# Batches 1 to 7 in units of all tokens by half of the expert features, with fixed engine orders and small pieces of work in the gaps

## The chip, the core and the metric

The kernel runs on one core of one Trainium2 chip. The metric is the device time of one execution in microseconds (us), from the first to the last instruction; the median of the runs is given. TensorE (PE) multiplies matrices and writes to PSUM, VectorE (DVE) does elementwise arithmetic, ScalarE (ACT) does activation functions and copies, GpSimd (POOL) and SyncE (SP) are used here for issuing DMA transfers. Every engine has a queue of its own and works through it in order; engines wait for one another by semaphores.

## The reference

An attention block with 8 batches and 8 heads (512 tokens, 32 states, 64 features a head) makes 544 rows of 512 per batch; an expert block with 2048 features follows. All is float32 on the chip (the expert weights come as float64 and are converted there).

```python
scores = scale * np.matmul(x, state.transpose(0, 1, 3, 2))       # tokens read states
a = softmax(scores); xread = np.matmul(a, state)
scores2 = scale * np.matmul(state, x.transpose(0, 1, 3, 2))      # states read tokens
a2 = softmax(scores2); sread = np.matmul(a2, x)
attn = np.concatenate([xread, sread], axis=2)                     # (8, 8, 544, 64)
x = attn.transpose(0, 2, 1, 3).reshape(4352, 512)
h = x @ w_in                                                      # (4352, 2048)
sp = np.maximum(h, 0.0) + np.log1p(np.exp(-np.abs(h)))            # softplus
g = h * erf(sp)
return g @ w_out                                                  # (4352, 512)
```

## The kernel before

For tokens, h is computed as (a) times (state x w_in): the small product `m` = state x w_in ("mixing") is made per batch, so that the contraction has only 256 (8 heads x 32 states). Batch 0 is done with plain products while the weights arrive; batches 1 to 7 and the state rows (called batch 8 here) use the seven-product scheme of Strassen and Winograd, at both products. The core below is that of batches 1 to 7. A batch has four passes: two halves of the tokens (h) by two halves of the features (g). One pass of `hidden7` takes 256 of the 512 tokens as a 2x2 block scheme whose blocks have 128 tokens, so each of its matmuls has 128 columns:

```python
def hidden7(b, g, h, between, copy=nc.scalar.copy):
    hs = act.tile([P, 4, S], F32, name="hs")
    s = act.tile([P, 4, S], F32, name="s")
    c11, c12, c21, c22 = (hs[:, k] for k in range(4))
    m1, u2, u3 = s[:, 3], c12, c21
    def product(n, bank, first=True):
        x, y = X[b, g][n - 1], Ys[b][n - 1]
        for i in range(GF):                                   # GF = 4 blocks of 128 features
            q = slice(P * i, P * i + P)
            ...  # matmul(out=bank[:, q], lhsT=x[:, q], rhs=y[:, h])     128 x 128
    p, q = (ps_h.tile([P, S], F32, name="h") for _ in range(2))
    product(1, p);  copy(m1, p)
    product(6, q);  add(u2, m1, q)
    between()
    product(2, p, False);  copy(c11, p)
    product(7, q, False);  add(u3, m1, q);  softplus(0)
    between()
    p, q = (ps_h.tile([P, S], F32, name="h") for _ in range(2))
    product(5, p);  add(c22, u3, p)
    product(4, q);  add(c21, u3, q)
    between()
    marks[:] = product(3, p, False), add(c12, u2, p)
    for k in (3, 2, 1):
        softplus(k)
    return s, hs

def finish(s, hs, parts=(slice(0, GF),)):
    nc.scalar.activation(out=s, in_=s, func=ACTF.Erf)
    for k in parts:
        nc.vector.tensor_tensor(s[:, k], s[:, k], hs[:, k], op=ALU.mult)
```

`between()` puts a piece of the pass before, its second product, between the pieces of the first. That second product (`project7`, matmuls of 256 columns) adds the two feature halves up in PSUM, over two passes, and `store7` evicts after the second:

```python
def project7(gT, hs, g, first, last, acc, order=range(7)):
    ...  # four VectorE sums of 128x512, 7 products of 4 matmuls 128x256,
         # accumulated in acc[0..3] over the two passes (first, last)

def store7(acc, put):
    ...  # 1 ScalarE copy, 2 VectorE adds of 128x512 and 3 of 128x256, 3 transfers out
```

The attention of the next batch is a generator that is stepped at set places of the passes. Its transposed scores, its weights and a transposed copy of x (`xT`) have tiles of their own; `w_in` (all 8 pieces) stays on chip. The order on VectorE and ScalarE in batches 1 to 8 is chosen by the scheduler (batch 0 is fixed by `in_order`).

Of the kernel before, what the change touches and what calls it, by code (L numbers as in the profile page):

```python
# [16 lines left out]
def kernel(  # L17
# [17 lines left out]
    nc = tc.nc  # L35
# [29 lines left out]

    x_t = {}
# [11 lines left out]
    def in_order(begun):  # L78

        last = {}  # L80
        for i in nc.cur_bb.bb.instructions[begun:]:
            if i.engine in last:
                tc.add_manual_dep(i, last[i.engine].name, mybir.DependencyInfo(
                    mybir.DependencyClass.NoSync, mybir.DependencyReason.DATA), reason="in_order")
            if i.engine in (nc.tensor.engine, nc.vector.engine, nc.scalar.engine,
                            nc.sync.engine):
                last[i.engine] = i
# [34 lines left out]
    w_in = const.tile([P, NF // 2, NK, 2 * P], F32, name="w_in")  # L122
# [31 lines left out]
    def weights_in(j):  # L154
        return weight(w_in[:, j],
                      moe_w_in[:, 2 * P * j:2 * P * j + 2 * P].rearrange("(k p) f -> p k f", p=P),
                      (NK, 2 * P))
# [32 lines left out]
    def scored(b, xT):  # L190


        s2 = [ps_at.tile([P, S], F32, name="at") for _ in range(2)]
# [8 lines left out]
    def scores(b, xT):  # L202
        s2 = scored(b, xT)
        on_pe = marks.pop()
        sc = att.tile([P, 2, S], F32, name="sc")
        for e in range(2):
            last = nc.scalar.copy(sc[:, e], s2[e])
        marks[:] = last, on_pe
        return sc, last
# [127 lines left out]
    def turn_x(b):  # L337
        xT = att.tile([P, NI, S], F32, name="xT")
        last = nc.vector.transpose(out=xT.rearrange("p i t -> p (i t)"),
                                   in_=xq_t.pop(b).rearrange("p i m d -> p (i m d)"))  # L340
        if b + 1 < B:
            load_xq(b + 1)
        return xT, last

    def attention(b, xT=None):

        turned = []
        if xT is None:  # L350
            xT, *turned = turn_x(b)
        sc, _ = scores(b, xT)
        marks.extend(turned)
        yield
        both = att.tile([P, NI, S], F32, name="xT")
        a = states_weights(b, [sc[:, e] for e in range(2)], both)
        yield
        if b == 2:
            z1 = sums(a)
        else:  # L360
            m2 = largest(sc)
            yield
            z2 = weigh_tokens(sc, m2, both[:, 2:4])
            yield
            z1 = sums(a)
            inverse(z2)
            yield
        normalise(a, z1)
        for e in range(2):
            nc.vector.transpose(out=aT[b][:, e], in_=both[:, e])  # L370
        yield
        if b == 2:
            z2 = weigh_tokens(sc, largest(sc), both[:, 2:4])
            inverse(z2)

        nc.vector.transpose(out=both[:, 0:2], in_=both[:, 2:4])
        a2T = att.tile([P, 2, NC, P], F32, name="sc")
        blocks = both[:, 0:2].rearrange("p e (c m n) -> p m (e c) n", m=NI, n=Ns)
        rows = a2T.rearrange("p e c (i n) -> p i (e c) n", n=Ns)
        for m in range(NI):  # L380
            for i in range(NI):
                nc.sync.dma_start(out=rows[Ns * m:Ns * m + Ns, i],
                                  in_=blocks[Ns * i:Ns * i + Ns, m])
        yield
        read_tokens(b, a2T, z2, *((ps_h, "h") if 1 < b < B - 1 else ()))
        if b + 1 < B:
            load_x(b + 1)
        yield
# [8 lines left out]
    def mixed_pair(b, gs):  # L397

        for g in gs:
            m_t[b, g] = mix.tile([P, 2, gw], F32, name="m")  # L400
        ps = [[pool.tile([P, gw], F32, name=n) for _ in range(2)]
              for pool, n in ((ps_at, "at"), (ps_h, "h"))]
        for k, g in enumerate(gs):
            for i in range(NI):
                for e in range(2):
                    r, q = slice(D * e, D * e + D), slice(Ns * i, Ns * i + Ns)
                    nc.tensor.matmul(out=ps[k][e][q, :], lhsT=st[r, b, q],  # L407
                                     rhs=w_in[r, 2 * g:2 * g + 2, i, :], start=True, stop=True)
        for k in 0, 1:
            nc.scalar.copy(m_t[b, gs[k]][:, 0], ps[k][0])  # L410
            nc.vector.tensor_copy(m_t[b, gs[k]][:, 1], ps[k][1])

    def mixed_part(b, g, j, parts, copy0=nc.scalar.copy, copy1=nc.vector.tensor_copy):
        n = gw // parts
        mg = m_t[b, g][:, :, n * j:n * j + n]
        fs = slice(2 * g + j, 2 * g + j + 2 // parts)
        ps = [ps_at.tile([P, gw], F32, name="at")[:, 0:n] for _ in range(2)]
        for i in range(NI):
            for e in range(2):
                r, q = slice(D * e, D * e + D), slice(Ns * i, Ns * i + Ns)  # L420
                nc.tensor.matmul(out=ps[e][q, :], lhsT=st[r, b, q],  # L421
                                 rhs=w_in[r, fs, i, :], start=True, stop=True)
# [3 lines left out]
    def combine_m(b, g):  # L426
# [4 lines left out]
        S1, S2, S4 = (sx[:, k] for k in range(3))  # L431
        tt = nc.vector.tensor_tensor
        tt(S1, X21, X22, op=ALU.add)
        tt(S2, S1, X11, op=ALU.subtract)
        tt(X21, X11, X21, op=ALU.subtract)
        tt(S4, X12, S2, op=ALU.subtract)
        X[b, g] = X11, X12, S4, X22, S1, S2, X21

    def combine_s(g):


        (X11, X12), (X21, X22) = ([w_in[:, GF * g + 2 * j:GF * g + 2 * j + 2, 2 * k:2 * k + 2, :]
# [5 lines left out]
        tt(S1, X21, X22, op=ALU.add)  # L448
        tt(S2, S1, X11, op=ALU.subtract)
        tt(X21, X11, X21, op=ALU.subtract)  # L450
        tt(S4, X12, S2, op=ALU.subtract)
        X[B, g] = X11, X12, S4, X22, S1, S2, X21

    def combine_a(b):
# [9 lines left out]
        tt(T1, Y12, Y11, op=ALU.subtract)  # L464
        tt(T2, Y22, T1, op=ALU.subtract)
        tt(Y12, Y22, Y12, op=ALU.subtract)
        last = tt(T4, Y21, T2, op=ALU.subtract)
        Ys[b] = Y11, Y21, Y22, T4, T1, T2, Y12
        return last
# [3 lines left out]
    def hidden7(b, g, h, between, copy=nc.scalar.copy):  # L473
# [4 lines left out]
        hs = act.tile([P, 4, S], F32, name="hs")  # L478
        s = act.tile([P, 4, S], F32, name="s")
        c11, c12, c21, c22 = (hs[:, k] for k in range(4))  # L480
        m1, u2, u3 = s[:, 3], c12, c21

        def product(n, bank, first=True):
            x, y = X[b, g][n - 1], Ys[b][n - 1]
            for i in range(GF):
                q = slice(P * i, P * i + P)
                if b < B:
                    ops = [(x[:, q], y[:, h])]
                else:
                    ops = [(x[:, i // 2, k, P * (i % 2):P * (i % 2) + P], y[:, k])  # L490
                           for k in range(2)]
                for k, (lhsT, rhs) in enumerate(ops):
                    last = nc.tensor.matmul(out=bank[:, q], lhsT=lhsT, rhs=rhs,  # L493
                                            start=(first and i == 0 and k == 0),
                                            stop=(i == GF - 1 and k == len(ops) - 1),
                                            skip_group_check=not first)
            return last

        def softplus(k):
            nc.scalar.activation(out=s[:, k], in_=hs[:, k], func=ACTF.Softplus)  # L500
        add = lambda o, x, y: nc.vector.tensor_tensor(o, x, y, op=ALU.add)  # L501
        p, q = (ps_h.tile([P, S], F32, name="h") for _ in range(2))
        product(1, p)
        copy(m1, p)  # L504
        product(6, q)
        add(u2, m1, q)
        between()
        product(2, p, False)
        copy(c11, p)  # L509
        product(7, q, False)  # L510
        add(u3, m1, q)
        softplus(0)
        between()
        p, q = (ps_h.tile([P, S], F32, name="h") for _ in range(2))
        product(5, p)
        add(c22, u3, p)
        product(4, q)
        add(c21, u3, q)
        between()
        marks[:] = product(3, p, False), add(c12, u2, p)  # L520
        for k in (3, 2, 1):
            softplus(k)
        return s, hs

    def hidden(b, fts, copies=(nc.vector.tensor_copy,) * 4):

        hs = act.tile([P, 4, S], F32, name="hs")
        s = act.tile([P, 4, S], F32, name="s")  # L530
        banks = []
        for i, f in enumerate(fts):
            hp = ps_h.tile([P, S], F32, name="h")
            for e in range(2):
                on_pe = nc.tensor.matmul(
                    out=hp, lhsT=m_t[b, f // GF][:, e, P * (f % GF):P * (f % GF) + P],
                    rhs=aT[b][:, e], start=(e == 0), stop=(e == 1))
            banks.append((nc.scalar.activation(out=s[:, i], in_=hp, func=ACTF.Softplus),
                          copies[i](hs[:, i], hp), on_pe))
        return s, hs, banks  # L540

    def finish(s, hs, parts=(slice(0, GF),)):
        nc.scalar.activation(out=s, in_=s, func=ACTF.Erf)  # L543
# [59 lines left out]

    def store7(acc, put):
        twice = lambda t: t.unsqueeze(1).to_broadcast([P, 2, E2])
        two = lambda t: t.rearrange("p (c e) -> p c e", c=2)
        m1, u3 = (outs.tile([P, E2], F32, name=n) for n in ("m1", "u3"))
# [13 lines left out]
    def put_x(b, h):  # L621
        rows = out[TB * b:TB * b + S].rearrange("(c p) e -> c p e", p=P)

        def go(r, ot, c=slice(0, d_model)):
            nc.sync.dma_start(out=rows[2 * h + r][:, c], in_=ot[:, c])
# [16 lines left out]

    def fast(b, parts, put):
        for h in range(parts):
            box = []

            def project_(gT, k, g, h, box):
                if k == 0:
                    box.extend(tiles(4))
                yield from project7(*gT, g, k == 0, k == 1, box,  # L650
# [361 lines left out]
```

## Time and profile before

| | before |
|---|---|
| median of 3 runs | 732.25 us (732.15 to 732.46) |
| span of the profiled execution | 730.7 us |
| granted TensorE clock | 1.00 |
| ACT_TABLE_LOAD, each | 1283 ns |
| DMA, HBM read and written | 33.03 MB and 8.91 MB |

The page lists for each engine its busy time and how many instructions it ran; PE has one row for matmuls and one (PEld) for loading their weights. The chain is followed back from the last instruction: at each step to what released it. A group line is "line engine operation out<-in shapes count | busy us, mean ns of one | idle time before it". In the timeline a line is "start us, length us, engine, line, operation, out<-in, count", and neighbours of one kind are merged; SPq is SyncE's queue, where the length is the time of issuing and not of the transfer.

### The profile page before, as it was taken

The page shows a single profiled execution, that of the slowest core. Times are in us where ns is not written, and L with a number is a line of the kernel's source. Part 1 is how long each engine was busy: PE and PEld are TensorE (multiplying, and loading weights), DVE is VectorE, ACT ScalarE, POOL GpSimd, SP SyncE. Part 2 cuts the span into 40 slices and gives each one's busy share as a digit, 9 for nine tenths or more (in the row PEclk, how much of TensorE's full clock was granted, in tenths as well). Part 3 has the DMA queues.
Part 4 walks back from the last instruction along what each step waited for, and adds up shares of the span by engine and source line. Part 5 has one row for each costly group of instructions (what it writes and reads, how often), then busy time and mean ns, then how long its engine had stood idle before and what let it go on. Part 6 is the DMA issues. An engine that isn't in the chain of part 4 may idle for free.

```text
span 730.7 us, 12128 instructions
## 1 busy us (share of the span) xinstructions
PE 721.6 (99%) x5016; PEld 588.0 (80%) x5016; DVE 524.0 (72%) x766; ACT 395.6 (54%) x498; POOL 0.7 (0%) x6
## 2 busy tenths in 40 slices
PE   8899999999999999999999999999999999999998
PEld 7434435889889888988989888988898899999996
DVE  4988887997798677867587669866686756674423
ACT  4898894665556444754455445544575434443340
POOL 0000000000000000000000000000000000000000
PEclk9999999999999999999999999999999999999999
DMA  7577842330153203310061104220111000000001
GB/s 234 174 216 241 224 94 58 87 59 30 19 99 67 50 1 66 80 30 30 1 144 27 33 1 94 60 44 9 38 50 30 30 1 30 1 30 1 30 1 29
DMA packets 139166, 46.40 MB, mean 64 GB/s; under 512 B 126696, under 2 KB 130536, under 8 KB 139112
## 3 DMA queue, kind: packets, MB, share of 16 engines
q1 hardware_dynamic: 136840, 44.92, 24.6%
q10 hardware_dynamic: 2272, 0.72, 0.5%
q8 instruction: 39, 0.64, 0.4%
q14 instruction: 15, 0.12, 0.1%
HBM read 33.03 MB, written 8.91 MB: 57 GB/s over the span
## 4 chain that ended last, share of the span: by engine, by line
PE 92%; DVE 2%; ACT 1%; issue 0%; ACTq 0%
PE o L600 50%; PE h L493 27%; PE o L550 7%; PE at L407 2%; PE h L407 1%; PE h L714 1%; PE at L197 1%; PE at L421 1%; PE h L277 1%; DVE s L727 0%; PE at L277 0%; DVE hs L721 0%; ACT L724 0%; DVE w_out L148 0%; ACT s L724 0%
## 5 line engine op out<-in xcount | busy, mean ns | idle before, releaser
L600 PE MATMUL o<-w_out,s 128*128 128x256 f32 x480 | 118.0, 380 | 0.0
L600 PE MATMUL o<-raw,hs 128*128 128x256 f32 x480 | 117.3, 382 | 0.0
L500 ACT ACTIVATE s<-hs 128x512 f32<-128x512 f32 x120 | 75.4, 630 | 74.3 <-DVE hs L501 74.0
L600 PE MATMUL o<-w_out,hs 128*128 128x256 f32 x480 | 114.1, 380 | 0.0
L600 PEld LDWEIGHTS o<-raw,hs 128*128 128x128 f32 x480 | 89.9, 190 | 22.6 <-issue 10.9
L501 DVE TENSOR_TENSOR hs<-hs,h 128x512 f32<-128x512 f32 x90 | 61.8, 687 | 62.6 <-PE h L493 62.4
L600 PEld LDWEIGHTS o<-w_out,hs 128*128 128x128 f32 x480 | 90.8, 190 | 16.3 <-issue 4.2
L600 PEld LDWEIGHTS o<-w_out,s 128*128 128x128 f32 x480 | 84.6, 191 | 7.9
L501 DVE TENSOR_TENSOR hs<-s,h 128x512 f32<-128x512 f32 x60 | 41.1, 685 | 67.6 <-PE h L493 67.1
L493 PEld LDWEIGHTS h<-aT,m 128*128 128x128 f32 x672 | 83.8, 192 | 4.3 <-issue 1.4
L493 PE MATMUL h<-aT,m 128*128 128x128 f32 x672 | 84.4, 275 | 0.0
L545 DVE TENSOR_TENSOR s<-s,hs 128x2048 f32<-128x2048 f32 (+1 forms) x31 | 68.8, 2218 | 20.4 <-ACT s L543 20.4
L504 ACT COPY s<-h 128x512 f32<-128x512 f32 x29 | 17.0, 585 | 107.7 <-PE h L493 107.7
L550 PE MATMUL o<-w_out,s 128*128 128x512 f32 x128 | 59.1, 600 | 0.6 <-DVE s L727 0.5
L493 PE MATMUL h<-sy,sx 128*128 128x128 f32 x448 | 59.4, 275 | 0.0
L493 PEld LDWEIGHTS h<-sy,sx 128*128 128x128 f32 x448 | 56.7, 192 | 2.1 <-issue 0.5
L543 ACT ACTIVATE s<-s 128x2048 f32<-128x2048 f32 x30 | 57.4, 1912 | 0.3
L509 ACT COPY hs<-h 128x512 f32<-128x512 f32 x29 | 17.0, 585 | 74.8 <-PE h L493 74.8
L600 PE MATMUL o<-raw,s 128*128 128x256 f32 x240 | 56.8, 379 | 0.0
L550 PEld LDWEIGHTS o<-w_out,s 128*128 128x128 f32 x128 | 23.1, 190 | 31.1 <-issue 25.8
L600 PEld LDWEIGHTS o<-raw,s 128*128 128x128 f32 x240 | 43.5, 190 | 4.7
L500 ACT ACT_TABLE_LOAD x31 | 39.8, 1283 | 0.5
(133 smaller groups left out, 915.4 us busy)
## 6 DMA issues: line engine op xcount, KB each, us to landing
raw<-in_moe_w_in_dram SPq DMA_DIRECT2D x8, 1024.0 KB, 5.7
raw<-in_moe_w_out_dram SPq DMA_DIRECT2D x8, 1024.0 KB, 4.8
xq<-in_x_dram SPq DMA_DIRECT2D x112, 64.0 KB, 2.2
x<-in_x_dram SPq DMA_DIRECT2D x56, 128.0 KB, 2.8
out_dram<-ot SPq DMA_DIRECT2D x18, 256.0 KB, 2.2
sc<-xT SPq DMA_DIRECT2D x112, 32.0 KB, 1.9
out_dram<-ot SPq DMA_DIRECT2D x28, 128.0 KB, 1.9
x<-in_x_dram ACTq DMA_DIRECT2D x2, 256.0 KB, 5.7
```

What stands on the lines that cost most here:

```text
L197: on_pe = nc.tensor.matmul(out=s2[e][q, :], lhsT=st[r, b, q], rhs=xT[r, i, :], start=True, stop=True)
L277: nc.tensor.matmul(out=sr[q, e, :], lhsT=a2T[:, e, c, q], rhs=xt[:, c, 2 * i + e, :], start=(c == 0), stop=(c == NC - 1))
L407: nc.tensor.matmul(out=ps[k][e][q, :], lhsT=st[r, b, q], rhs=w_in[r, 2 * g:2 * g + 2, i, :], start=True, stop=True)
L493: last = nc.tensor.matmul(out=bank[:, q], lhsT=lhsT, rhs=rhs, start=(first and i == 0 and k == 0), stop=(i == GF - 1 and k == len(ops) - 1 ...
L500: nc.scalar.activation(out=s[:, k], in_=hs[:, k], func=ACTF.Softplus)
L501: add = lambda o, x, y: nc.vector.tensor_tensor(o, x, y, op=ALU.add)
L504: copy(m1, p)
L509: copy(c11, p)
L543: nc.scalar.activation(out=s, in_=s, func=ACTF.Erf)
L545: nc.vector.tensor_tensor(s[:, k], s[:, k], hs[:, k], op=ALU.mult)
L550: nc.tensor.matmul(out=acc[r], lhsT=gT[:, i, P * r:P * r + P], rhs=w_out[:, GF * g + i, :], start=(g == 0 and i == 0), stop=(g == NG - 1 a ...
L600: nc.tensor.matmul(out=acc[bank][:, E2 * c:E2 * c + E2], lhsT=lhs[:, i, :], rhs=rhs[:, g, i, :], start=(first and i == 0 and c == 0), stop ...
```

## The change

A batch now has two units, each of all 512 tokens by half of the features. In `hidden_wide` both token halves are columns of one matmul (2x128), and the seven products go twice over two of the four feature blocks. The results of a unit are two slots of a ring of three: the inner slot is projected at once, the outer one during the next unit. `project_wide` projects one slot for one half of the features and evicts it by itself; the second half of the features is added in DRAM by an accumulating transfer issued from GpSimd. The aim is fewer and longer matmuls in the first product and fewer changes of ScalarE's table. Room for the ring is made by keeping half of w_in on chip only: both halves are stored in DRAM (`kept_in`) at the end of batch 0, and one half at a time is brought back.

The orders of TensorE, VectorE and ScalarE are now those of the program text from batch 1 on. VectorE's other work (softmax, transposes, sums) is a queue of pieces, each with a cost (0.6 or 1.13), and `fill(budget)` takes pieces up to a budget between two steps of the first product.

Core of the diff (cut; `...` marks cuts):

```diff
-    w_in = const.tile([P, NF // 2, NK, 2 * P], F32, name="w_in")
+    ring = const.tile([P, 2, 3, GF, GF, P], F32, name="ring")
+    w_in = const.tile([P, NF // 4, NK, 2 * P], F32, name="w_in")
+    away = ring[:, :, 2]...                       # upper half of w_in, in slot 2 of the ring
+    kept_in = dram.tile([2, P, NF // 4, NK * 2 * P], F32, name="kept_in")
...
-        xT = att.tile([P, NI, S], F32, name="xT")      # turn_x: into another tile, one piece
+        xT = xq_t[b].rearrange("p i m d -> p i (m d)")  # in place, one or four pieces
...
+    def hidden_wide(b, g, low, between, fill, later):
+        view = lambda t: t.rearrange("p (h u) -> p h u", h=2)
+        for o in range(2):
+            s, hs = (... ring[:, u, low:low + 2, k, 2 * o:2 * o + 2] ...)
+            def product(n, bank, first=True):
+                out = bank.rearrange("p (h i t) -> p i h t", h=2, i=2)
+                for i in range(2):
+                    q = P * (2 * o + i)
+                    nc.tensor.matmul(out=out[:, i], lhsT=x[:, q:q + P], rhs=y, ...)  # 2x128 columns
+            p, q = bank(), bank()
+            product(1, p);  nc.scalar.copy(m1, view(p))
+            if late: late(1)
+            product(6, q);  add(u2, m1, view(q))
+            if o or not later: between()
+            fill(1.8)
+            product(2, p, False);  nc.scalar.copy(c11, view(p))
+            if not o and later: between()
+            product(7, q, False);  add(u3, m1, view(q));  softplus(0)
+            between();  fill(1.2)
+            p, q = (ps_at.tile([P, S], F32, name="at") for _ in range(2))
+            product(5, p);  add(c22, u3, view(p))
+            product(4, q);  softplus(3);  add(c21, u3, view(q))
+            between();  fill(0.6 if o else 1.2)
+            product(3, p, False);  softplus(2);  add(c12, u2, view(p))
+            fill(0 if o else 1.2)
+            late = softplus
+        late(1)
...
+    def project_wide(n, g, put, more):
+        ...  # 7 products of 4 matmuls 128x256 in two banks; per slot and half of the features
+        ...  # 2 ScalarE copies 128x256, 4 VectorE adds 128x256, 1 of 128x512, 2 transfers out
+        put(1, o2, more=more) ... put(0, o1, more=more)
...
-            nc.sync.dma_start(out=rows[2 * h + r][:, c], in_=ot[:, c])
+            if more:
+                nc.gpsimd.dma_start(out=rows[2 * h + r][:, c], in_=ot[:, c], accum_op=ALU.add)
+            else:
+                nc.sync.dma_start(out=rows[2 * h + r][:, c], in_=ot[:, c])
...
+    nc.sync.dma_start(out=kept_in[0], in_=w_in...)             # 2 MB
+    for u in range(2):
+        nc.sync.dma_start(out=kept_in[1][:, 2 * u:2 * u + 2], in_=away[:, u]...)   # 1 MB each
...
+    bring(1)                                       # w_in <- kept_in[1]
+    for n, (b, u) in enumerate((b, u) for b in range(1, B) for u in range(2)):
+        low = 1 - n % 2;  inner, outer = 1, 2 * low
+        ...                                        # queue the unit's small pieces (add_jobs)
+        hidden_wide(b, o, low, lambda: next(steps, None), fill, n == 0)
+        erf_part(inner, outside) ... erf_part(inner, inside)
+        ...                                        # the rest of the pending projection meanwhile
+        times_part(inner, outside);  times_part(inner, inside)
+        finish_on_act(slot(outer)[0])
+        for k, _ in enumerate(project_wide(inner, o, put[1 - low], u)):
+            ...                                    # k == 5: read tokens, mixing, next scores
+            ...                                    # then bring(...) of the other half (u == 0)
+        def pending(...): return project_wide(outer, o, put, u)
...
-            store(acc, lambda r, ot: put_x(0, r // 2)(r % 2, ot))    # batch 0: after all of it
+            ot = outs.tile(...); nc.scalar.copy(ot, acc[r]); put_x(0, r // 2)(r % 2, ot)  # each row block
...
+    in_order(begun, [nc.tensor, nc.vector, nc.scalar])
```

Two mixings of batch 1 and four of batch 0's last matmuls move from before the first unit to within it. By shape, the lists of instructions of the two programs compare as follows:

| | before | after |
|---|---|---|
| PE matmul, 128 columns | 984 | 200 |
| PE matmul, 2x128 columns | 0 | 392 |
| PE matmul, 256 columns | 840 | 840 |
| PE, other shapes | 704 | 704 |
| ACT table loads | 90 | 54 |
| DVE two-operand, 128x2048 | 29 | 0 |
| DVE two-operand, 128x1024 and 128x2x512 | 20 | 78 |
| DVE two-operand, 128x512 and 128x2x256 | 396 | 396 |
| DVE two-operand, 128x256 | 69 | 139 |
| DVE transposes, 2048, 1024 and 512 | 7, 7, 32 | 1, 0, 70 |
| GpSimd transfers out, accumulating | 0 | 28 |

## The prediction

> **What bounds the kernel now.** I read the page's busy shares first, then its chain, then the groups by shape, and last the timeline around the place where batch 1 begins, because the change acts from there on.
>
> ```profile
> PE 721.6 (99%) x5016; PEld 588.0 (80%) x5016; DVE 524.0 (72%) x766; ACT 395.6 (54%) x498; POOL 0.7 (0%) x6
> PE 92%; DVE 2%; ACT 1%; issue 0%; ACTq 0%
> PE o L600 50%; PE h L493 27%; PE o L550 7%; PE at L407 2%; PE h L407 1%; PE h L714 1%; PE at L197 1%; PE at L421 1%; PE h L277 1%; DVE s L727 0%; PE at L277 0%; DVE hs L721 0%; ACT L724 0%; DVE w_out L148 0%; ACT s L724 0%
> ```
>
> TensorE is busy 99% of the span and is 92% of the chain; 77% of the chain is two lines, the second product (L600) and the first (L493). The stretch view of one whole steady batch says the same (columns: length, then busy us and count for PE, PEld, DVE, ACT, POOL, the clock, DMA share, GB/s):
>
> ```profile
> 324.30:404.00 79.70, 79.70 (x600) 69.43 (x592) 58.22 (x90) 41.58 (x53) 0.00 (x0) 1.00 0.22 47
> ```
>
> PE has no idle microsecond in it; VectorE has 21 us of room, ScalarE 38. So only fewer or shorter matmul slots can save time, and any new wait of PE adds to it in full. What one slot costs is read off starts, not off the mean durations (275 and 380 ns), which overlap:
>
> ```profile
> 119.17 1.05 PE L493 MATMUL h<-aT,m 128*128 128x128 f32 x8
> 120.06 1.06 PE L493 MATMUL h<-sy,sx 128*128 128x128 f32 x8
> 134.25 2.76 PE L600 MATMUL o<-w_out,s 128*128 128x256 f32 x12
> 136.85 0.61 PE L493 MATMUL h<-sy,sx 128*128 128x128 f32 x4
> ```
>
> Eight 128-column records take 120.06 - 119.17 = 0.89 us, 0.111 each (0.112 over the whole trace); twelve of 256 take 2.60 us, 0.216 each. One f32 matmul is two records (the program's list has 840 matmuls of 256 columns, the trace 1680 records on L600). Two matmuls of 128 columns thus cost 0.448 us, one of 256 columns 0.432 us. The wide form saves 4%, not half.
>
> **What the Trainium skill says.** "TensorE: Matmul & The Clock Gate", section Back-to-back issue gap: a gap is N/2.4 + 2.5 ns, so 55.8 for 128 and 109.2 for 256. The trace has exactly twice these for an f32 record, 112 and 216, so it agrees that only the 2.5 ns per instruction is saved. "VectorE: DVE Perf Modes", section The TRN2 errata: an f32 two-operand operation takes (N+151)/0.96 ns, 691 at 512. The trace has 687, and 0.60 from start to start when they stand back to back, which is what I use for load. "ScalarE: Activation LUTs", section What ACT_TABLE_LOAD costs: 1283 ns; the trace has 1283 in every group. "DMA: Bandwidth & Descriptors", section Anatomy of one DMA: a transfer issued from GpSimd takes 2.0 us plus bytes/436e3. No accumulating transfer is in this trace, so my estimate for the new 256 KB ones, 2.6 us, has only this page behind it.
>
> **The change part by part.**
> PE, first product: batches 1 to 7 have 7 x 112 = 784 matmuls of 128 columns; the list of the changed program has 392 of 2x128. Saved: 392 x (0.448 - 0.432) = 6.3 us. The second product keeps its 840 matmuls of 256 columns, the mixing, scores and reads keep theirs. The runs of 32-row matmuls (mixing, scores, reading) now stand together in two places of a batch and not three; going in costs some 0.1 us each time, so 0.1 to 0.2 us a batch, about 1 us in all. Together -7.3 us.
>
> VectorE: in a steady batch 64 operations of 512 become about 69, the four of 2048 become eight of 1024, and the additions of 256 go from 10 to 20. At 0.60, 2.20, 1.13 and 0.334 us: +3.0, +0.2, +3.3, less the big transposes now counted in the first (2.23 + 1.16): +3.1 us on 58.2. That is 61 of 79; it does not bind as a whole. ScalarE: 90 table loads become 54, 36 x 1.29 = -46 us, against more and smaller copies from PSUM. Neither is on the path.
>
> Order within a unit, worked through by hand with these costs, PE to VectorE 0.27 us after the last slot (121.22 in the trace for a group whose slots ended at 120.95): in the first product a sum must be done 1.73 us after its operand's matmuls end (two groups of four records later), and needs 0.27 + 0.69 + 0.1. With the small pieces the fuller unit (the second of a batch) has 26 operations of 512, two of 256 and five tiny ones in the 17.3 us of its two passes; the tightest place still has about 0.5 us of room. From the end of the first product, softplus, a table load, half of erf and the multiplication are done 5.4 us later; PE has four half-done products, 6.9 us, to fill that. The weighted sums come at 7.8 us and are needed at 8.6. I find no wait of PE in a steady unit, but with margins under 1 us.
>
> DMA, in place at the start: w_in now has room for half; its two halves (4.2 MB) are written to DRAM, and one half is read back per batch (2.1 MB, some 10 us at the 220 to 240 GB/s of the loading phase, a batch ahead of need). The first time is different. The upper half of w_in lies in the place ("away") in which unit 0 of batch 1 puts its results, so ScalarE's first eviction waits for the store of that half. The stores stand in SyncE's queue behind the loads of x and xq:
>
> ```profile
> 86.76 10.00 SPq L100 DMA_DIRECT2D xq<-in_x_dram  x16
> 96.85 4.28 SPq L72 DMA_DIRECT2D x<-in_x_dram  x8
> 111.68 11.63 SPq L382 DMA_DIRECT2D sc<-xT  x16
> ```
>
> In the changed program the loads of x come first, after batch 0's read (88.5 us), then xq, so the stores can be issued at 88.5 + 4.3 + 10.0 = 103 us. With 2 us of latency and 4.2 MB at 240 to 350 GB/s they land at 117 to 122.5 us, the first half of "away" at 114 to 118. Unit 0 begins earlier than before: from 119.17 are taken two mixings (1.02 us each, moved later) and four 512-column matmuls (0.86 each, moved into the unit), so 113.7 us. Its first sum would be wanted at 117.2; it comes 0.7 us after the stores. A stall of 1 to 6 us, and I take 3. The small transfers that move batch 1's token weights (sc<-xT, L382 before) then queue behind the read-back, and their issue takes 11.6 us; by my count they land at 135 to 138, just as PE comes to read them.
>
> Sum: 732.25 - 7.3 + 3 = 728 us.
>
> **The rivals.** (a) The stores are quick (large contiguous rows), no stall: 725 us. For it: 16 KB rows against 2 and 4 KB of the weight loads. Against: the queue position is fixed by order. (b) The fixed order of VectorE bites: one operation placed too early waits and holds all behind it. For it: margins under 1 us in each of 14 units, and VectorE 61 of 79 us. Each unit losing 0.5 us would make +7, so 735. Against: the pieces are sized to 0.6 and 1.13 us, which is just what the trace shows. (c) The accumulating transfers from GpSimd are slow; their source tiles are two deep, the next write comes some 6 to 8 us after issue. If one took 12 us, VectorE would stall about 5 us a batch, of which part reaches PE: 740 to 760. Against: estimate 2.6 us. (d) PE is bound and the wide form really saves more (weight loads no longer in the way): PEld is 0.19 us per load against 0.112 us per slot, but the starts show that loads are hidden already. Not more than the 6.3 us.
>
> **Range and chances.** The floor is 732.25 - 7.3 - 1 = 724, since nothing else shortens PE's own work; PE would need to lose 14.7 us to be 2% faster, and there isn't so much to take. Upwards there is the start (6 us) and 14 units with small margins. So 724 to 739 for 8 times in 10. Faster by over 2%: 0.02; slower by over 2% needs (c) or a broken unit: 0.07.
>
> **What would show it.** Right: L559 (the new first product) at 0.216 us per record and about 170 us in all; steady batches 78.6 us long with no PE idle in the stretch view; one gap of PE of some us at 114 to 123, released by an eviction that waited for a store of kept_in; VectorE near 545 us, ScalarE near 375. Wrong: gaps of PE in every unit released by VectorE (b), VectorE waiting for a DMA before the ot additions (c), or a batch that is still 79.7 us with PE full, which would mean that strided columns cost more per slot.

## The result, and the profile after

| | before | after |
|---|---|---|
| median of 4 runs | 732.29 us (732.15 to 732.46) | 729.98 us (729.88 to 730.04) |
| after / before | | 0.9968, 95% interval 0.9954 to 0.9982 |
| span of the profiled execution | 730.7 us | 728.0 us |
| one steady batch, from one read of the tokens to the next | 79.76 us | 79.15 us |
| ACT table loads | 90 | 54 |

The change saves 2.3 us, 0.3%. First the page of the kernel after: busy time, share and count of each engine, then the chain by engine and by line.

```profile
PE 716.6 (98%) x4232; PEld 562.0 (77%) x4232; DVE 546.0 (75%) x872; ACT 370.1 (51%) x536; POOL 25.2 (3%) x34
...
PE 80%; ACT 4%; DVE 3%; issue 1%; ACTq 0%; DVEq 0%
PE o L702 44%; PE h L559 13%; PE at L559 10%; PE h L604 3%; PE o L676 3%; PE h L442 2%; PE at L442 1%; ACT xT L390 1%; PE at L285 1%; PE o L626 1%; PE h L205 1%; DVE ring L1086 0%; DVE w_out L156 0%; ACT ring L838 0%; ACT ring L1082 0%
```

TensorE still bounds the kernel. Its share of the chain reads 80% and was 92%, but these two can't be compared as they stand: the chain is followed back only to 88.9 us here and to 26.3 us before, so the shares add up to 88 and to 96%. From 113 us on, where the change acts, TensorE has 580.6 of the chain's 611.5 us and had 613.7 of 614.1; VectorE has 10.8 and had 0.4; ScalarE has 16.4 and had none. The line to see is ACT xT L390, the exponentials of the next batch's softmax, which were not in that part of the chain before. One steady batch in the stretch view (length, then busy us and count for PE, PEld, DVE, ACT, POOL; clock, DMA share, GB/s):

```profile
341.35:420.50 79.15, 79.08 (x482) 65.90 (x481) 60.92 (x106) 38.30 (x58) 3.48 (x4) 1.00 0.39 87
```

By this view PE is idle for under 0.1 us, and yet the batch is only 0.61 us shorter. The busy time counts modelled ends of matmuls, so it hides small waits; the starts in the timeline show them. Here are the first product's records of 2x128 columns, and below them where a new wait begins:

```profile
402.27 1.89 PE L559 MATMUL h<-aT,m 128*128 128x256 f32 x8
404.00 1.03 PE L702 MATMUL o<-raw,ring 128*128 128x256 f32 x4
```

Eight records take 404.00 - 402.27 = 1.73 us, 0.216 each, exactly what a record of the second product takes. The new waits of PE are found in the timeline by the bracket, or by a start that lies behind the end of the slots before:

```profile
139.92 3.26 PE L702 MATMUL o<-raw,ring 128*128 128x256 f32 x14 [0.68 <-DVE ring L734]
180.81 1.99 PE L702 MATMUL o<-raw,ring 128*128 128x256 f32 x8 [0.58 <-ACT m L707]
305.52 2.75 PE L702 MATMUL o<-w_out,ring 128*128 128x256 f32 x12
308.11 1.89 PE L702 MATMUL o<-raw,ring 128*128 128x256 f32 x8
310.07 1.99 PE L702 MATMUL o<-w_out,ring 128*128 128x256 f32 x8
```

The bracket counts from the modelled end of the matmul before; from start to start the gaps are 0.85 us (unit 0 of batch 1), 0.75 (unit 1 of batch 1) and, in the last two lines, 310.07 - 308.11 = 1.96 us for eight records that need 1.73: a wait of 0.24. It has no bracket and is easily missed, but it comes back in the first unit of batches 3, 4, 5 and 6, each time with 0.10 us of issue behind it. ScalarE at the same place shows the reason:

```profile
305.91 1.28 ACT L388 ACT_TABLE_LOAD   x1
307.21 1.15 ACT L388 ACTIVATE xT<-xT 128x512 f32<-128x512 f32 x2
308.26 0.70 ACT L390 ACTIVATE xT<-sc,m 128x512 f32<-128x512 f32 x1
308.88 0.19 ACT L390 ACTIVATION_READ_ACCUMULATOR xT<-sc,m 128x1 f32 x1
308.97 0.71 ACT L390 ACTIVATE xT<-sc,m 128x512 f32<-128x512 f32 x1
309.58 0.19 ACT L390 ACTIVATION_READ_ACCUMULATOR xT<-sc,m 128x1 f32 x1
309.67 0.35 ACT L719 COPY ot<-o 128x256 f32<-128x256 f32 x1
```

The table load and the exponentials (3.8 us) stand ahead of the copy of c11 (L719) in ScalarE's fixed order, though c11's product, the end of the group of twelve, was done at 308.27 (305.52 + 2.75). The copy reads one half of a PSUM bank, the product S4 x B22 writes the other half, and it starts at 310.07, just behind the copy. The Trainium skill ("PSUM — Partial Sum Buffer", section PSUM bank collisions raise a hardware error) says that two engines must not be in one bank and quadrant at once, and that the compiler's scheduler puts a dependency between two such instructions; the wait here agrees, and no run shows what would happen without it. So a copy whose result nobody needs yet can still hold TensorE.

Last, the store of w_in. SyncE's timeline:

```profile
102.49 0.49 SPq L1019 DMA_DIRECT2D kept_in<-w_in  x1
103.02 1.37 SPq L1021 DMA_DIRECT2D kept_in<-ring  x2
113.98 0.32 SPq L1067 DMA_DIRECT2D w_in<-kept_in  x1
```

and ScalarE's first eviction into the place that is being stored:

```profile
114.14 0.59 ACT L565 COPY ring<-h 128x512 f32<-128x512 f32 x1 [4.44 <-PE h L559]
```

The read-back at 113.98 had to wait for the stores, so 4.2 MB were down 11.5 us after the first issue, 365 GB/s with all latency. The eviction at 114.14 waited for PE and not for a store: no stall. The transfers (KB each, median us from issue to landing):

```profile
w_in<-kept_in SPq DMA_DIRECT2D x7, 2048.0 KB, 8.5
...
out_dram<-ot SPq DMA_DIRECT2D x32, 256.0 KB, 2.2
...
out_dram<-ot POOLq DMA_DIRECT2D x28, 256.0 KB, 4.5
```

An accumulating transfer takes twice as long to land as a plain one of the same size.

Set against the prediction's sum, the profiles before and after give the table below. All terms are read from starts of PE. A run of 32-row matmuls has a cost at its edges too, as in the kernel before:

```profile
362.31 1.89 PE L600 MATMUL o<-raw,hs 128*128 128x256 f32 x8
364.13 1.10 PE L277 MATMUL h<-x,sc 128*32 128x64 f32 x64
...
366.19 1.99 PE L600 MATMUL o<-w_out,hs 128*128 128x256 f32 x8
368.02 1.89 PE L600 MATMUL o<-raw,hs 128*128 128x256 f32 x8
```

From 362.31 to 364.13 and from 366.19 to 368.02 eight records take 1.82 and 1.83 us where 1.73 is usual: 0.09 us going in, 0.10 coming out.

| term, us | predicted | measured |
|---|---|---|
| wide form, 392 matmuls | -6.3 | -5.6 (mean pitches 111.6 and 216.0 ns) |
| runs of 32-row matmuls with their edges | -1 | -0.9 (from 20 us on, 33 runs became 23) |
| stall behind the stores | +3 | 0 |
| waits of PE over 0.15 us, from batch 1 on | 0 | +3.1 (none before, eight after) |
| the same before batch 1 | not named | -0.3 |
| pieces under 0.15 us, 0.7 of them behind these waits | not named | +1.1 |
| sum | -4.3 | -2.6 (profiled spans 730.7 and 728.0; medians -2.3) |

### The profile page after: what moved, and what is told of

It reads as the page before. It is cut to its first block, busy times and chain, and to the rows that moved or that the text cites. A ratio compares the mean times of both kernels' runs of the same rounds, so it can differ in the third digit from the quotient of the medians.

```text
span 728.0 us, 10875 instructions
## 1 busy us (share of the span) xinstructions
PE 716.6 (98%) x4232; PEld 562.0 (77%) x4232; DVE 546.0 (75%) x872; ACT 370.1 (51%) x536; POOL 25.2 (3%) x34
## 4 chain that ended last, share of the span: by engine, by line
PE 80%; ACT 4%; DVE 3%; issue 1%; ACTq 0%; DVEq 0%
PE o L702 44%; PE h L559 13%; PE at L559 10%; PE h L604 3%; PE o L676 3%; PE h L442 2%; PE at L442 1%; ACT xT L390 1%; PE at L285 1%; PE o L626 1%; PE h L205 1%; DVE ring L1086 0%; DVE w_out L156 0%; ACT ring L838 0%; ACT ring L1082 0%
## 5 line engine op out<-in xcount | busy, mean ns | idle before, releaser
L702 PE MATMUL o<-w_out,ring 128*128 128x256 f32 x896 | 209.5, 381 | 0.4
L702 PEld LDWEIGHTS o<-w_out,ring 128*128 128x128 f32 x896 | 168.4, 190 | 35.6 <-DVE uv L686 5.5
L702 PE MATMUL o<-raw,ring 128*128 128x256 f32 x672 | 161.3, 380 | 1.3 <-DVE ring L734 0.7
L702 PEld LDWEIGHTS o<-raw,ring 128*128 128x128 f32 x672 | 127.1, 190 | 19.9 <-issue 1.1
L552 ACT ACTIVATE ring<-ring 128x512 f32<-128x512 f32 x112 | 70.6, 631 | 61.5 <-DVE ring L542 60.9
L1086 DVE TENSOR_TENSOR ring<-ring 128x1024 f32<-128x1024 f32 x60 | 71.8, 1221 | 20.9 <-ACT ring L1082 16.9
L559 PE MATMUL h<-aT,m 128*128 128x256 f32 x336 | 82.2, 380 | 0.1
L542 DVE TENSOR_TENSOR ring<-ring,at 128x512 f32<-128x512 f32 x84 | 57.0, 679 | 14.8 <-PE at L559 13.1
L626 PE MATMUL o<-w_out,ring 128*128 128x512 f32 x128 | 59.0, 599 | 0.6 <-DVE ring L841 0.5
L565 ACT COPY ring<-h 128x512 f32<-128x512 f32 x28 | 16.4, 586 | 64.0 <-PE h L559 64.0
L626 PEld LDWEIGHTS o<-w_out,ring 128*128 128x128 f32 x128 | 23.5, 190 | 29.4 <-issue 24.4
L574 ACT COPY ring<-h 128x512 f32<-128x512 f32 x28 | 16.4, 588 | 47.0 <-PE h L559 47.0
L734 DVE TENSOR_TENSOR ring<-ring 128x512 f32<-128x512 f32 x56 | 38.6, 689 | 1.4
L735 DVE TENSOR_TENSOR ring<-ring 128x512 f32<-128x512 f32 x56 | 36.2, 683 | 0.0
```

The costliest lines, as they stand in the source:

```text
L552: nc.scalar.activation(out=s[k], in_=hs[k], func=ACTF.Softplus)
L559: nc.tensor.matmul(out=out[:, i], lhsT=x[:, q:q + P], rhs=y, start=(first and i == 0), stop=(i == 1), skip_group_check=not first)
L626: nc.tensor.matmul(out=acc[r], lhsT=gT[:, i, P * r:P * r + P], rhs=w_out[:, GF * g + i, :], start=(g == 0 and i == 0), stop=(g == NG - 1 a ...
L702: nc.tensor.matmul(out=out, lhsT=lhs[:, i, :], rhs=rhs[:, g, i, :], start=(start and i == 0), stop=(i == GF - 1), skip_group_check=not start)
L734: return [lambda: tt(S1, A21, A22, op=ALU.add), lambda: tt(S2, S1, A11, op=ALU.subtract), lambda: tt(S3, A11, A21, op=ALU.subtract), lambd ...
L735: lambda: tt(S3, A11, A21, op=ALU.subtract), lambda: tt(S4, A12, S2, op=ALU.subtract)]
```

## The experiments

Each is the changed kernel with one edit; gaps are from start to start, as above.

**The wide form alone undone.**

```diff
-  nc.tensor.matmul(out=out[:, i], lhsT=x[:, q:q + P], rhs=y, ...)
+  for h in range(2):
+      nc.tensor.matmul(out=out[:, i, h], lhsT=x[:, q:q + P], rhs=y[:, h], ...)
```

> The changed kernel, but every matmul of 2x128 columns in the first product of batches 1 to 7 is split again into two of 128. Theory A (the gain of the wide form is only the fixed cost of an instruction, two records of 112 ns against one of 216): 784 records pairs x 8 ns = +6.3 us against the changed kernel, 736.3 us, all of it on PE, 0.9 us a batch. Rival B (the wide form also takes weight loads out of PE's way, or its two-part columns cost extra): clearly more than 7 us, or clearly less than 5. Rival C (narrow slots give VectorE more room and the new waits shrink): 4 to 5.5 us.

Measured 735.3 us (735.0 to 735.38), 5.3 more than after; to before 1.0041 (1.0027 to 1.0054). Its steady batch:

```profile
343.37:423.36 79.99, 79.92 (x593) 69.64 (x593) 61.11 (x106) 38.30 (x58) 3.49 (x4) 1.00 0.38 86
```

79.99 - 79.15 = 0.84 us a batch, 5.9 in seven, though the whole run grew by 5.3 only. That lies in the range of rival C, but not for its reason: the eight waits of PE over 0.15 us are all there, 3.0 us in sum against 3.1. Where the other half microsecond lies is open. So the width is worth 5.3 to 5.9 us, a little less than the 6.3 of the rounded pitches, and the rest of the change costs 735.3 - 732.3 = 3 us by itself.

**The exponentials behind the copies.**

```diff
-  if n == 1: soft[2][1]()                    # exponentials ahead of the projection
+  if k == 1 and n == 1: soft[2][1]()         # behind the copy of m1
...
-  if k == 5 and ...:                         # steady, first unit
-      soft[b + 1][1]()
+  if k == 9 and steady and u == 0 and b + 1 < B: soft[b + 1][1]()   # behind the copy of c11
```

> The changed kernel, with the four exponentials of the next batch's softmax moved behind one copy on ScalarE: in the first batch's second unit behind the copy of m1, in the first unit of batches 3 to 6 behind the copy of c11. Theory A (these exponentials, 3.9 us in one piece, hold a copy for which PE waits: 0.75 us once, 0.24 us four times): -1.7 us against the changed kernel, and the gaps of PE there are gone. Rival B (PE waits there for something else, or the exponentials then delay the next unit): between -0.5 and +2 us.

Measured 727.97 us (727.79 to 728.13), 2.0 less than after; to before 0.9942 (0.9929 to 0.9954). ScalarE and PE at the place shown above:

```profile
307.92 0.37 ACT L719 COPY ot<-o 128x256 f32<-128x256 f32 x1 [2.45 <-PE o L702]
308.31 1.28 ACT L388 ACT_TABLE_LOAD   x1
```

```profile
307.67 1.89 PE L702 MATMUL o<-raw,ring 128*128 128x256 f32 x8
309.40 1.89 PE L702 MATMUL o<-w_out,ring 128*128 128x256 f32 x8
```

The copy now waits for PE, not PE for the copy, and eight records again take 1.73 us. All four gaps of 0.24 and the 0.75 are gone. One of 0.50 came up at 187 us, where PE waits for VectorE's sum of ot behind a softmax piece. No work was removed; only the place of the exponentials changed, in five units, on an engine that is half idle.

**One multiplication earlier in unit 0 of batch 1** (the 0.85 us gap).

```diff
   if n == 0:
       done(steps)
+      times_part(inner, outside)
       excursion(1, ...)                      # read, mixing, scores
-  times_part(inner, outside)
```

> The changed kernel, with the first multiplication of the first unit of batch 1 put on VectorE ahead of the two copies of the mixing. Theory A (PE's gap of 0.85 us there comes of VectorE doing two copies, then two multiplications, then two sums in a row): -0.85 us. Rival B (erf is late and not the copies): 0.

Measured 730.25 us (730.01 to 730.58): no gain. The 0.85 us gap went, and this came:

```profile
136.64 1.09 PE L442 MATMUL at<-w_in,st 64*32 64x512 f32 x14 [0.97 <-DVE st L291]
```

The multiplication waits for erf, and in VectorE's fixed order the small step that the mixing needs (L291) now stands behind it. The wait was moved to the next consumer.

**Four waits at once**: the two edits above, and both outer multiplications of the last unit at k == 5 and not 3.

> The two edits before together, and in the last unit of batch 7 the outer slot's multiplications two steps later (a gap of 0.26 us). Theory A (the named waits are separate and each in full on PE's path): -1.7 - 0.85 - 0.26 = -2.8 us, 727.2 us. Rival B (what is saved is given back at the next wait): less than half of it, 728.6 us or more.

Measured 729.53 us (729.51 to 729.61). In the last unit the 0.26 us gap became one of 1.54:

```profile
658.95 1.99 PE L702 MATMUL o<-raw,ring 128*128 128x256 f32 x8 [1.38 <-DVE ot L686]
```

Both multiplications now stand ahead of the sum of ot. Again the wait was moved, not removed.

**Plain transfers from SyncE, one read-back.** The addition of the two halves in DRAM is left out, and later batches use whichever half of w_in is on chip.

```diff
-  if more: nc.gpsimd.dma_start(..., accum_op=ALU.add)
-  else:    nc.sync.dma_start(...)
+  nc.sync.dma_start(...)
...
-  bring(1 - begins(b + 1))
+  (no transfer)
```

> The changed kernel without the two new kinds of transfer in the steady batches: the 28 accumulating transfers become plain ones from SyncE's queue, so the second half of the features overwrites the first instead of being added, and the halves of w_in are read back only once, so that from batch 2 on one mixing uses the wrong half. Both leave out part of the computation, none of PE's, VectorE's or ScalarE's work. Theory A (all of these transfers are hidden): within 0.3 us of 729.98. Rival B (they cost something, by contention or by holding the output tiles): 1 us or more faster.

Measured 739.77 us (739.45 to 740.09), 9.8 more than after and not what I had expected. One gap holds nearly all of it. VectorE and SyncE there:

```profile
236.79 0.69 DVE L686 TENSOR_TENSOR ot<-uv,o 128x512 f32<-128x512 f32 x1 [8.52 <-DMA out_dram<-ot]
```

```profile
224.03 3.15 SPq L102 DMA_DIRECT2D xq<-in_x_dram  x6
227.22 0.49 SPq L1064 DMA_DIRECT2D w_in<-kept_in  x1
227.82 16.61 SPq L761 DMA_DIRECT2D out_dram<-ot  x4
```

The stores stand in SyncE's queue behind the loads of x and xq, so the two tiles of ot come free late; in the kernel after, GpSimd issues them at 221.62. A part of the loss is TensorE's clock (see the end).

**Plain transfers from GpSimd, one read-back**, to part the queue from the kind of transfer: the same edit, but nc.gpsimd.dma_start without accum_op. The same things are left out.

> The 28 second halves go out by plain transfers, but from GpSimd's queue as in the changed kernel, and w_in is read back only once; the addition of the two feature halves is left out, and later batches use the wrong half of w_in. Theory A (accumulating and reading back are hidden; what cost 9.8 us in the run with SyncE's queue was the place in that queue): 730.0 us within 0.4, the 8.6 us gap at 229 gone. Rival B (the plain form itself, or the missing read-back, moves SyncE's other transfers and opens a gap): 733 to 740.

Measured 729.94 us (729.71 to 730.01), the time of after. The plain form lands in 2.5 us and not 4.5:

```profile
out_dram<-ot POOLq DMA_DIRECT2D x28, 256.0 KB, 2.5
```

So accumulation and read-back are hidden entirely, and what the run before lost was the place in SyncE's queue.

**The stores twice.**

```diff
+  for again in range(2):
       nc.sync.dma_start(out=kept_in[0], in_=w_in...)
       for u in range(2): nc.sync.dma_start(out=kept_in[1][...], in_=away[:, u]...)
```

> The changed kernel with the stores of w_in to DRAM at the end of batch 0 done twice, 8.4 MB instead of 4.2. Theory A (the first unit does wait for these stores, and it is only their speed, some 400 GB/s in the trace and not 240, that hid them): they land near 125 us and not 114, the first sum comes 9 us later, +8 to +10 us, with one gap of PE between 114 and 126 us. Rival B (the first unit doesn't depend on them in time, or the rest of batch 1 absorbs the delay): under +2 us.

Measured 739.38 us (738.94 to 739.98), 9.4 more. The stall that the prediction feared, in full:

```profile
121.62 0.58 ACT L565 COPY ring<-h 128x512 f32<-128x512 f32 x1 [11.93 <-DMA kept_in<-ring]
```

```profile
122.26 2.08 PE L559 MATMUL h<-aT,m 128*128 128x256 f32 x4 [7.30 <-ACT ring L565]
```

The dependency is real; with single stores the transfers are just quick enough.

**Only TensorE's order fixed; then TensorE's and VectorE's.**

```diff
-  in_order(begun, [nc.tensor, nc.vector, nc.scalar])
+  in_order(begun, [nc.tensor])               # first run;  second: [nc.tensor, nc.vector]
```

> The changed kernel with only TensorE's order fixed in batches 1 to 8; VectorE's and ScalarE's orders are the scheduler's choice again. Theory A (the fixed orders carry the change: VectorE has 61 of 79 us to do and a margin under 1 us per unit, so a different order must make PE wait): +5 to +40 us. Rival B (the wide units would do without; what the fixed order costs is the waits found): 727 to 731 us.

> Only TensorE's and VectorE's orders are fixed, the scheduler orders ScalarE. Freeing both had cost 36.5 us, with TensorE waiting for VectorE's sums. Theory A (it is VectorE's order that matters; ScalarE has half its time free): 729 to 735 us. Rival B (ScalarE's order matters as much, since TensorE waits for its copies and each misplaced activation can add a table load of 1.28 us): 745 us or more, with more than 54 table loads and gaps of TensorE released by ScalarE.

The first took 766.49 us (765.49 to 767.16), 36.5 more than after; the second 743.1 us (743.05 to 743.29), 13.1 more. PE's waits in the first (us in total, times, longest):

```profile
PE o L702 <- DVE ring L734: 12.3, 11, 1.3
PE h L559 <- DVE ring L542: 5.3, 1, 5.3
```

In the second, ScalarE at the end of a first product:

```profile
414.91 1.28 ACT L1082 ACT_TABLE_LOAD   x1
416.20 1.06 ACT L1082 ACTIVATE ring<-ring 128x1024 f32<-128x1024 f32 x1
417.28 1.28 ACT L552 ACT_TABLE_LOAD   x1
418.58 1.15 ACT L552 ACTIVATE ring<-ring 128x512 f32<-128x512 f32 x2
...
420.00 1.28 ACT L1082 ACT_TABLE_LOAD   x1
421.30 1.06 ACT L1082 ACTIVATE ring<-ring 128x1024 f32<-128x1024 f32 x1
```

The scheduler starts half of erf as soon as its operands are there, then goes back to softplus: two more table loads, 90 in all as before the change. The second half of erf ends late, VectorE's multiplication waits for it, and PE for the sums (up to 1.2 us). A steady batch takes 81.2 us. Four more waits of 0.95 us are PE's for the copy of c11 (L719), which now stands behind half of erf. So it is rival B in kind, though 743.1 lies just under its 745: ScalarE's order is worth 13 us, with half of ScalarE's time free.

**No small pieces in the gaps** from batch 3 on; all of them in the second product.

```diff
   def fill(budget):
+      if late_only[0] and budget < 99: return
```

> The changed kernel with no small pieces in the gaps from the first unit of batch 3 on: everything queued for a unit is done in one go in the middle of the inner projection (a place that exists already for what is left over). Theory A (the pieces are what keeps PE fed): in the second unit of a batch the transfer of the token weights is then issued only about 1 us before the read, so PE waits its 11 us of issue and 2 us of landing, and in both units 5 to 11 us of VectorE work stand in one block: +10 to +20 us a batch for four batches, 770 to 810 us. Rival B (VectorE's room elsewhere takes it): under +5 us.

Measured 846.5 us (845.38 to 849.04), 116 more, outside what I expected. PE and SyncE in a steady batch:

```profile
367.72 2.29 PE L285 MATMUL at<-x,sc 128*32 128x64 f32 x64 [18.65 <-DMA sc<-xT]
```

```profile
355.77 10.39 SPq L414 DMA_DIRECT2D sc<-xT  x16
```

The pieces end in the 16 transfers that carry the next batch's weights. Late pieces mean late issues, 10.4 us of issuing, and PE waits 18.7 us for them, in four batches; six waits of up to 5.1 us for VectorE's uv come on top, and a mean clock of 0.943 (see the end). The run tells how much of the design rests on the gaps, not which of two theories is right.

**The waits out**: the run with the exponentials late, and two pieces of VectorE's work moved by single steps.

```diff
+  spare = n == 1 or (b == B - 1 and u == 1)
-  if k == 3: all_of(after)                                    # both multiplications
+  if k == 3: after.pop(0)()
+  if k == (5 if b == B - 1 and u else 3): all_of(after)       # the second, in the last unit
-  rest({..., 6: 1, 7: 0, ...})
+  rest({..., 6: int(not spare), 7: int(spare), ...})
```

> The exponentials behind the copies as in the run that did only that (727.97), and in two units less VectorE work ahead of the sum that TensorE waits for: in unit 1 of batch 1 and in the last unit of batch 7 one small piece goes one step later, and in the latter one outer multiplication goes two steps later. Theory A (each wait is the place of one operation in a fixed order): the 0.50 us gap at 187 and the 0.26 us gap at 657 go, 727.2 us. Rival B (a piece put later makes the next wait, as with both multiplications moved): 727.9 to 728.5, with a new gap within 5 us of the old.

Measured 726.97 us (726.92 to 727.29); to before 0.9929 (0.9916 to 0.9941), the fastest of all. The gaps at 187 and 657 are gone, and no new one of over 0.1 us came. Its steady batch has PE busy from end to end:

```profile
340.30:419.11 78.81, 78.81 (x482) 65.99 (x481) 60.94 (x106) 38.42 (x58) 3.48 (x4) 1.00 0.39 88
```

**And the wait in unit 0 of batch 1**: in addition, ScalarE makes the first mixing copy with half of erf behind it, and the last two evictions of batch 0 go into the next projection.

```diff
-  (nc.vector.tensor_copy if both and not k else nc.scalar.copy)(m_t[b, g][:, 0], ps[k][0])
+  nc.scalar.copy(m_t[b, g][:, 0], ps[k][0])
+  if amid and not k: amid()                  # half of erf
...
+  if k == 2 and n == 0: all_of(held)         # evictions of row blocks 2 and 3
```

> The kernel with those waits out, and in unit 0 of batch 1 ScalarE, not VectorE, makes the first of the two mixing copies, half of erf stands behind it, and the evictions of batch 0's last two row blocks are deferred into the next projection. Theory A: VectorE reaches the sums 0.6 us earlier, the 0.85 us gap at 139 shrinks to 0.2, 726.6 us. Rival B (ScalarE's queue is now what binds there: its copies free the banks for the scores, or half of erf is too late for the second multiplication): 727.2 or more, with a gap of TensorE between 135 and 141 released by ScalarE.

Measured 729.2 us (728.25 to 730.42). VectorE reached the sums 0.5 us earlier, but so did PE, and the gap only went from 0.85 to 0.75. The late evictions cost more. VectorE next, and SyncE:

```profile
150.37 0.69 DVE L688 TENSOR_TENSOR ot<-uv,o 128x512 f32<-128x512 f32 x1 [3.42 <-DMA out_dram<-ot]
```

```profile
139.56 8.40 SPq L102 DMA_DIRECT2D xq<-in_x_dram  x16
148.05 0.91 SPq L766 DMA_DIRECT2D out_dram<-ot  x2
```

The two stores missed their place ahead of the loads of x and xq, so ot came free 13 us later, and PE stood 2.7 us. The time is in rival B's range, but neither theory had named this reason, although the plain transfers from SyncE had shown the same trap.

## Why the prediction was right, and where not

The time (728.0 said, 729.98 measured) lies in the range, 2 us off, but that it came so near is partly luck: a stall of 3 us was counted that did not come, and 3.1 us of waits came that were not counted.

- "Saved: 392 x (0.448 - 0.432) = 6.3 us": right in kind, 0.4 to 1 us too large. The wide record's pitch is 0.216 us, and undoing the form costs 5.3 us (5.9 from a steady batch). 0.112 is 0.1116 rounded up, which is 0.6 us over 1568 records. The trace is also not "exactly twice" the cited gap at both widths: twice 55.8 ns is 111.6, but twice 109.2 is 218.4 against 216.0 measured. A wide record saves 7.2 ns on two narrow ones, and the formula would give 4.8, so the reading that "only the 2.5 ns per instruction is saved" does not hold. Rival (d) falls.
- "The runs of 32-row matmuls ... about 1 us in all": right, -0.9. The runs themselves grew from 5.81 to 5.89 us a batch (the scores alone from 1.02 to 1.09; why was not tried), but two pairs of edges instead of three save 0.20. With edges a steady batch has 6.40 us of them before and 6.29 after.
- "A stall of 1 to 6 us, and I take 3": 0. The dependency was right, as doubling the stores shows. The mis-sized term is the rate: 240 to 350 GB/s and 2 us of latency were assumed, the stores made 365 with latency. That their larger rows are the reason was not tried. Rival (a) described this start, but not the 725 us that it named.
- "I find no wait of PE in a steady unit, but with margins under 1 us": this is the step that failed. My count by hand followed VectorE's sums, the operands of PE. It left out that PE's next product also waits for ScalarE's copy out of the same bank, and that the exponentials stand ahead of that copy. Of the 3.1 us of new waits these are 1.7 (four times 0.24, and the 0.75 in unit 1 of batch 1), 2.2 with the 0.10 of issue behind each. Moving the exponentials took all five away and gained 2.0, one new wait of 0.50 included, so this is shown. The other 1.4 are VectorE's, in units that carry extra work and that my steady count did not cover: 0.85 and 0.26 in unit 0 of batch 1, 0.26 in the last unit of batch 7.
- Rival (b), the fixed order: the right mechanism at half the size, 3.1 us over 14 units (0.22 each, not 0.5), and on ScalarE as well as VectorE. But the fixed order of the two engines is worth 36 us: with it come these small waits, without it much larger ones.
- "Neither is on the path", of VectorE and ScalarE: wrong for the waits above, which are theirs. A table load (305.91) even heads the 3.8 us that hold the copy of c11, and in the run with ScalarE free two more loads inside a unit reach PE. ScalarE at half load was no proof of slack at each place.
- Rival (c): refuted. Accumulating transfers land in 4.5 us, longer than the 2.6 us of the estimate (2.5 for a plain one), and cost nothing: with plain ones from the same queue the kernel takes 729.94 us, and neither VectorE nor ScalarE has a wait for a store of ot in the trace after.
- VectorE "near 545", ScalarE "near 375": 546.0 and 370.1. Batches of 78.6: 79.15, and 78.81 with the waits out.

So the expected gain was there, and about half of it was given back in waits of 0.2 to 0.9 us. With the order changed in three kinds of unit (first units of batches 3 to 6, unit 1 of batch 1, last unit of batch 7) it is 726.97 us, 5.3 us less than before. The 0.85 us in unit 0 of batch 1 stayed open: two attempts on it gained nothing.

## What to carry to other kernels

When an order is fixed by hand, go through every wait of the bounding engine, also for the engine that only empties its PSUM banks: a copy behind a long activation holds the next product into that bank, however idle the engine is on average. Moving one instruction in a fixed order can move the wait to whatever stands behind it: here three moves gained and three gave it back, and the timeline of the next 5 us shows which. A store that frees a tile should not stand in a queue behind a block of loads that takes 8 us to issue.

## What the hardware showed that I had not expected

- After a long gap TensorE runs slow for some time. In the run with plain transfers from SyncE the eight records behind the 8.4 us gap took 3.58 us from the start of the first to the next group, 0.45 each and not 0.216:

```profile
237.53 3.78 PE L702 MATMUL o<-raw,ring 128*128 128x256 f32 x8 [8.43 <-DVE ot L686]
241.11 2.44 PE L702 MATMUL o<-w_out,ring 128*128 128x256 f32 x8
```

  The granted clock is 0.50 from 237.55 to 241.95, and from 243.39 on four records take 0.86 us again. The mean clock of that run was 0.992; with the doubled stores it was 0.995, and without small pieces 0.943. Behind the wait of 2.7 us in the last run above the clock stayed at 1.00. The Trainium skill ("TensorE: Matmul & The Clock Gate", section What's actually happening) has the clock halve after an idle window of some 3.4 us, which agrees; such a wait costs more than its own length.
- An accumulating transfer of 256 KB from GpSimd takes 4.5 us to land, a plain one from the same queue 2.5, from SyncE 2.2.
